# Layer 1 of the first 1024 tokens on x not divided by its rms

## The chip, the cores and the metric

The kernel runs on one core of one Trainium2 chip. The metric is the time of one execution in microseconds (us) on the device. The engines are named as in the profile: PE is TensorE's matmul, PEld its weight load, DVE is VectorE, ACT is ScalarE, POOL is GpSimd, SP is the engine whose queue issues all DMAs here.

## What is computed

Three steps follow one another, on 4 batches of 576 tokens (2304 tokens in all, 512 features):

```python
scores = q @ k.T / sqrt(64)          # 8 heads of 64
# heads 0..3: the 32 latest keys; heads 4..7: every 32nd key; both causal
x = softmax(masked(scores)) @ v      # as 2304 x 512
rms = sqrt(mean(x * x, axis=-1) + 1e-6)
xn = x / rms * rms_g
g = xn @ w_gate                      # layer 1: 512 -> 1536
x = (g * sigmoid(g) * (xn @ w_val)) @ w_out
h = x @ w_in                         # layer 2: 512 -> 2048
out = softplus(h) @ w_out2
```

Because the division by rms is one number per token, a gate product of undivided x can be divided after the product, before the sigmoid; the value product enters the result of layer 1 linearly, so its division can wait until the end of layer 1.

## The kernel before

**Layout.** x is held transposed, features on the partitions and tokens along the free axis, in `xs`. The tokens are cut into five chunks, `CUTS = (0, 512, 1024, 1536, 2048, 2304)`. Side 0 is chunks 0 and 1 (1024 tokens, `TA`), side 1 is chunks 2, 3 and 4. Layer 1 runs over side 0, then over side 1; layer 2 follows in the same order.

**Products.** Each float32 operand is split into a high part h (a ScalarE copy to fp32r) and a low part l = x - h (a subtraction on VectorE or GpSimd); a product is three matmuls, h·h, h·l and l·h, of 128x128 by 512 columns (`mm3`, L434). `split_op` splits x into the operand tile `ob` (L351, L355); `direct(c)` does that for the four feature blocks of a chunk. The weights come as 64-bit floats: `decode` loads 512 KB into one of two `raw` tiles and turns it into float32 with one ScalarE and three VectorE instructions (L370 to L376; L373 is the last reader of `raw`), `prep_in` and `prep_out` split it into `win` and `wout`.

**Layer 1 of side 0.** For each f (12 blocks of 128 of the 1536 hidden units) and each chunk, `plain` makes a gate and a value product of twelve matmuls each into two PSUM banks; `chain1` makes silu on ScalarE (L867) from the gate's bank into a tile of the ring `gv`, multiplies it on VectorE with the value's bank (L868), and `halves` splits the result into the rings `gh`/`gl`. `out1` multiplies a pair of f's with `wout` and adds into `xs` on VectorE (L901; for the first pair a ScalarE copy, L899). `combine` and `build` make the operands of side 1 (`tb`, `ob`), where some products are saved by sums of operands (`quad`).

**The statistics.** `stats(c)` squares the four feature blocks on ScalarE (L452), sums them over the partitions with four products with a matrix `ones` (L453), and makes 1/rms from Ln and Exp on ScalarE (L457, L458) and three VectorE steps (L459, L461, L462) in `ssq`. For chunks 0 and 1 `norm` then multiplies x by `rms_g` and by 1/rms on VectorE (L472), ahead of the splits. For chunks 2 to 4 the squares are gathered while the attention delivers x, `rms_g` is put on at that place, and `norm` runs after.

**The order.** All instructions are collected with their dependencies and costs by `pr.add`, and a planner (`Program.emit`, `Trial`) writes the order on each engine's queue, by due times that it works back from PE's order. It chooses VectorE or GpSimd for elementwise operations on SBUF (`two`), and ScalarE or VectorE for some copies (`evict`). There are two such plans: the first covers the attention and f = 0 to 9 of side 0 (`DEALT = 10`), the second everything after.

The attention of batches 0 and 1 is written first (`attend`, units 0 to 15). Within it, at step 12, `early` calls for the statistics of chunk 0, its splits, and the products of f = 0 for it; the products of f = 1 follow. Then come silu and the first `out1`, the table for Exp and Ln again, `stats(1)`, the table for silu, and layer 1 of chunk 1. The attention of batches 2 and 3 is a list of small steps (`steps`) that `side_a` deals out between the products of f = 0 to 9; each group of four units has one `turn`, in which ScalarE switches to the Exp table, makes the exponentials, and switches back. The second of the turns takes the statistics of chunk 2 with it.

**Rings.** `gv` has two tiles of its own; for the dealt part two more are lent to it, the two halves of `ssq` for chunks 0 and 1, which nothing needs after the division.

Of the kernel before, what the change touches and what calls it, by code (L numbers as in the profile page):

```python
# [10 lines left out]
F32 = mybir.dt.float32  # L11
# [14 lines left out]
KD = DM // 128  # L26
# [10 lines left out]
W1N, W2N = DFF // 128, DF2 // 128  # L37
DEALT = 10
LT, LT2, LV, EB = 4, 4, 5, 5
WARM = 9  # L40
# [207 lines left out]
def attn_glu_softplus(  # L248
# [16 lines left out]
    def all_of(key):  # L265
        return (key, 0, 1 << 30)
# [20 lines left out]
    def dma(kb, fn, r, w):  # L287
        pr.add("SP", 650, fn, r, w, kb=kb)
# [59 lines left out]
    def split_op(src, ksrc, slot, k, n0=0, eng="POOL"):  # L348
# [3 lines left out]
        sub(eng, n, l, src, h.bitcast(F32), [ksrc, kh], [kl])  # L352

    def two(eng, n, name, o, x, y, r, w):
        pr.add("DVE", 68 + n / 0.96, lambda: getattr(nc.vector, name)(o, x, y), r, w,  # L355
               alt=(110 + n * 2.3, lambda: getattr(nc.gpsimd, name)(o, x, y)))
# [3 lines left out]

    hold = []

    def decode(src, t, kt, keep):

        raw, kraw = raws.next()
        u, ku = cvu.next()
        words = raw.bitcast(U32).rearrange("p (n two) -> p n two", two=2)
        wlo, whi = words[:, :, 0], words[:, :, 1]
        dma(512, lambda: nc.sync.dma_start(out=raw, in_=src), hold, [kraw])
        act(512, lambda: nc.scalar.activation(t, whi.bitcast(F32), AF.Copy, scale=2.0 ** -112), [kraw], [kt])  # L370
        dve(512, lambda: nc.vector.tensor_scalar(out=u, in0=t.bitcast(U32), scalar1=0x80000000, scalar2=None,
                                                 op0=ALU.bitwise_and), [kt], [ku], True)
        dve(512, lambda: nc.vector.scalar_tensor_tensor(  # L373
            out=u, in0=wlo, scalar=29, in1=u, op0=ALU.logical_shift_right, op1=ALU.bitwise_or),
            [kraw, ku], [ku])
        dve(512, lambda: nc.vector.scalar_tensor_tensor(  # L376
            out=t.bitcast(U32), in0=t.bitcast(U32), scalar=3, in1=u,
            op0=ALU.logical_shift_left, op1=ALU.bitwise_or), [kt, ku], [kt])
        dma(256, lambda: nc.sync.dma_start(out=wk[keep], in_=t), [kt], [("wk", keep, keep + 1)])

# [59 lines left out]
    def stats(c, ring_):  # L440
# [5 lines left out]
        for i, kk in enumerate((0, 2, 1, 3) if c < 2 else (0,)):  # L446
            y, ky = r, kr
            if c < 2:
# [14 lines left out]
                                                       op0=ALU.add, op1=ALU.mult), [kr, ks], [kr])  # L463
        if c < 2:
            norm(c, "DVE")
# [12 lines left out]
    def attention(at, use):  # L478
# [5 lines left out]
        mask = at.tile([128, MW], BF16, name="mask")  # L484
        dma(100, lambda: nc.sync.dma_start(out=mask, in_=masks), [], [all_of("mask")])
        vb = ring(at, "vb", 2, [128, 9, 128])
        eb = ring(at, "eb", EB, [128, 5 * LK])
        pp = ring(at, "pp", 2, [128, 6, 128])
        pt = ring(at, "pt", 4, [128, 3 * 128])
        sq = ring(at, "sq", 2, [128, 6 * SK])  # L490
        mz = ring(at, "mz", 8, [128, 2, 6])
# [29 lines left out]
        def load_v(u):  # L521
            b, p, t0, n = units[u]
            kp, nt = (LK, 9) if p < 2 else (128, 6)
            vt, (kv, _, _) = vb.next()
            src = vl[b, p] if p < 2 else vs[b, p - 2]
            vals[u // 2] = (vt, kv)
            dma(nt * (48 if p < 2 else 50), lambda: nc.sync.dma_start(out=vt[:kp, :nt, :], in_=src), [], [all_of(kv)])

# [118 lines left out]
        def stage_v(u):  # L647
# [8 lines left out]
            for a in range(n):  # L656
                t, kt = pts[a // 3]
                for h in range(2):
                    o = (2 * (a % 3) + (h ^ (u % 2))) * nq
                    pr.add("PE", 59, lambda a=a, h=h, o=o, t=t: nc.tensor.matmul(  # L660
                        xb[64 * h:64 * h + 64, a * nq:(a + 1) * nq], lhsT=vt[r0:r1, v0 + a, 64 * h:64 * h + 64],
                        rhs=t[r0:r1, o:o + nq], start=True, stop=True), [all_of(kv), kt],
                        [kx], mode=1 if loc else 3)
# [72 lines left out]
    def steps(at, after, ring_):  # L736
# [3 lines left out]
        def turn(us, cs):  # L740
            table(EXP_LN)
            rest = [at.e(u) for u in us]
            for c in cs:
                stats(c, ring_)
            table("silu_and_others")
            for fn in rest:
                fn()
            for c in cs:
                norm(c, "POOL")

# [108 lines left out]

    def chain1(gate, val, n=CH, r4=False, eng="POOL"):  # L860
        (gb, kg), (vb_, kv) = gate, val
        if "bank" in kg[0]:
            a, ka = fk["gv"].next()
        else:
            a, ka = gb, kg
        a, gb, vb_ = a[:, :n], gb[:, :n], vb_[:, :n]
        act(n, lambda: nc.scalar.activation(a, gb, AF.Silu), [kg], [ka], True)  # L867
        dve(n, lambda: nc.vector.tensor_mul(a, vb_, a), [kv, ka], [ka])  # L868
        return halves(a, ka, n, eng, r4)
# [108 lines left out]
    with tc.manual_schedule():  # L978
# [9 lines left out]
        def direct(c):  # L988
            slots = (B11, B21) if c % 2 == 0 else (B12, B22)
            for kk in range(KD):  # L990
                x, kx = xview(kk, CUTS[c], CUTS[c + 1])
                split_op(x, kx, slots[kk // 2], kk % 2, eng="DVE" if kk % 2 or c and kk < 3 else "POOL")

        gates = {}

        def half(f, c, ring_):
            gates[f, c] = [plain(w_at(f, 0), row, c, ring_) for row in (0, 1)]

        def early():
            use.s = s_banks  # L1000
            stats(0, f_banks)
            direct(0)
            half(0, 0, f_banks)

        def prepare(f, parts, u):
# [13 lines left out]

        dma(64, lambda: nc.sync.dma_start(out=id_sb, in_=ident), [], [all_of("id")])  # L1020
        dma(2, lambda: nc.sync.dma_start(out=rg_sb, in_=rg), [], [all_of("rg")])
# [13 lines left out]
        def side_a(f, queue):  # L1035
# [4 lines left out]
            for c in (0, 1) if f > 1 else (1,):  # L1040
# [5 lines left out]
                step(queue)  # L1046
                g[f, c] = chain1(gate, val, eng="DVE" if f < DEALT else "POOL")
                drain(1 if f < W1N - 1 else 0)
# [4 lines left out]
        with ExitStack() as c2:  # L1053
# [7 lines left out]
            for f in (0, 1):  # L1061
                g[f, 0] = chain1(*gates.pop((f, 0)))
            o_banks.t = f_banks.t
# [5 lines left out]
            o_banks.keys = {}  # L1069
            table(EXP_LN)  # L1070
            stats(1, t_banks)
            table("silu_and_others")
            direct(1)
            half(0, 1, v_banks)
            tv = Ring(banks.t[2:4], "bank", 2)
            use.t = use.v = tv
            for i in (0, 1):
                fk["gv"].keys[len(fk["gv"].t)] = ("ssq", i * CH, i * CH + CH)
                fk["gv"].t.append(ssq[:, i * CH:i * CH + CH])
            queue, last_turn = steps(x, {1: (2,)}, tv)  # L1080
            o_banks.t = banks.t[4:6]
# [3 lines left out]
            prep1(DEALT, 0)  # L1085
            pr.emit()
        o_banks.t = banks.t[4:6] + banks.t[2:4]
        o_banks.keys = {i: (f"bank{i}", 0, 1 << 20) for i in (2, 3)}
# [5 lines left out]
        for f in range(DEALT, W1N):  # L1094
            side_a(f, [None, None, (last_turn,)] if f == DEALT else [])
            if f == DEALT:
                combine(*SIDES[1][:2], False)
        drain(len(todo))
        o_banks.t, o_banks.keys = banks.t[4:], {}
        build(*SIDES[1], False)  # L1100
# [117 lines left out]
```

## Time and profile before

| | us |
|---|---|
| median of 3 runs | 901.63 (901.39 to 902.55) |
| the profiled execution | 900.52 |
| its span, first to last instruction | 898.7 |
| PE busy in the span | 882.7 |
| VectorE busy | 712.9 |
| ScalarE busy | 486.1 |
| GpSimd busy | 28.1 |

The rows of the profile are read from one execution; its time is its span and what lies around it. Matmuls overlap, so a busy PE says that PE had no hole, not that it did its most.

### The profile page before, as it was taken

How to read it: one execution, taken by the hardware profiler on the slowest of the kernel's cores; microseconds unless marked ns; L12 is line 12 of the kernel's file. 1: busy time of each engine (PE TensorE's matmuls, PEld its weight loads, DVE VectorE, ACT ScalarE, POOL GpSimd, SP SyncE). 2: the span in 40 equal slices, each digit the busy share in tenths (PEclk: the TensorE clock that was granted, in tenths of full speed). 3: DMA queues.
4: the chain of work that ended last, by engine and by line, in shares of the span. 5: the costliest groups of instructions: out<-in, count | busy, mean ns of one | idle time of the engine just before them, and what ended most of it. 6: DMA issues, size and time to landing. Idle time of an engine off the chain costs nothing.

```text
span 898.7 us, 14075 instructions
## 1 busy us (share of the span) xinstructions
PE 882.7 (98%) x5320; PEld 725.7 (81%) x5320; DVE 712.9 (79%) x1349; ACT 486.1 (54%) x999; POOL 28.1 (3%) x26
## 2 busy tenths in 40 slices
PE   7899999999999999999999999999999999999998
PEld 6567777778777888888888888888888888888886
DVE  4988898998599995888988799877798456676644
ACT  5987664545364675444545567544474655434331
POOL 0000010200000000000100100000000000000000
PEclk7999999999999999999999999999999999999999
DMA  7874667363040443344553025321114111111003
GB/s 254 263 228 146 205 205 224 124 214 106 13 141 23 151 152 105 134 146 140 183 154 104 2 85 178 137 71 48 47 47 153 36 47 48 47 32 39 1 1 117
DMA packets 41858, 102.18 MB, mean 114 GB/s; under 512 B 4800, under 2 KB 5568, under 8 KB 41792
## 3 DMA queue, kind: packets, MB, share of 16 engines
q1 hardware_dynamic: 41792, 101.31, 35.5%
q8 instruction: 41, 0.67, 0.3%
q14 instruction: 25, 0.20, 0.1%
HBM read 78.74 MB, written 22.54 MB: 113 GB/s over the span
## 4 chain that ended last, share of the span: by engine, by line
PE 67%; DVE 3%; issue 0%
PE bank L434 67%; DVE xs L901 1%; DVE ob L355 0%; DVE tb L355 0%; DVE xs L355 0%; DVE win L355 0%; DVE w L355 0%; DVE ssq L355 0%; DVE glx L355 0%; DVE xs L919 0%; DVE gv L355 0%; DVE ssq L868 0%; DVE gv L868 0%; DVE gl L355 0%
## 5 line engine op out<-in xcount | busy, mean ns | idle before, releaser
L434 PE MATMUL bank<-ob,win 128*128 128x512 f32 (+1 forms) x1560 | 430.8, 360 | 2.7 <-ACT ob L351 1.8
L434 PEld LDWEIGHTS bank<-ob,win 128*128 128x128 f32 x1560 | 283.4, 188 | 55.0 <-ACT ob L351 2.2
L434 PE MATMUL bank<-tb,win 128*128 128x512 f32 x672 | 232.8, 392 | 0.0
L434 PEld LDWEIGHTS bank<-tb,win 128*128 128x128 f32 x672 | 125.4, 188 | 22.9 <-DVE xs L901 0.4
L919 DVE TENSOR_TENSOR xs<-bank,xs 128x512 f32<-128x512 f32 x126 | 86.8, 689 | 45.7 <-PE bank L434 44.4
L405 ACT ACTIVATE win<-w 128x512 fp32r<-128x512 f32 (+1 forms) x136 | 83.4, 616 | 63.9 <-PE bank L434 32.7
L355 DVE TENSOR_TENSOR win<-w,win 128x512 fp32r<-128x512 f32 (+1 forms) x134 | 89.5, 673 | 15.6 <-ACT win L405 12.6
L434 PE MATMUL bank<-wout,ghx 128*128 128x512 f32 x304 | 100.0, 390 | 0.0
L434 PE MATMUL bank<-wout,gh 128*128 128x512 f32 x272 | 90.4, 390 | 0.0
L434 PE MATMUL bank<-ghx,wout 128*128 128x512 f32 x224 | 84.1, 394 | 0.0
L434 PE MATMUL bank<-gh,wout 128*128 128x512 f32 (+1 forms) x256 | 81.3, 356 | 0.5 <-DVE xs L901 0.4
L901 DVE TENSOR_TENSOR xs<-bank,xs 128x512 f32<-128x512 f32 (+1 forms) x100 | 62.2, 628 | 8.9 <-PE bank L434 8.1
L434 PEld LDWEIGHTS bank<-wout,ghx 128*128 128x128 f32 x304 | 56.9, 188 | 11.7
L434 PEld LDWEIGHTS bank<-wout,gh 128*128 128x128 f32 x272 | 50.9, 188 | 10.6
L816 ACT ACTIVATE gv<-bank 128x512 f32<-128x512 f32 x48 | 28.4, 592 | 48.1 <-PE bank L434 47.6
L434 PE MATMUL bank<-wout,glx 128*128 128x512 f32 x152 | 53.2, 389 | 0.0
L434 PEld LDWEIGHTS bank<-gh,wout 128*128 128x128 f32 x256 | 45.5, 189 | 9.0 <-DVE xs L901 1.4
L434 PEld LDWEIGHTS bank<-ghx,wout 128*128 128x128 f32 x224 | 41.9, 188 | 8.4 <-ACT ghx L856 0.2
L434 PE MATMUL bank<-wout,gl 128*128 128x512 f32 x136 | 47.7, 389 | 0.0
L373 DVE SCALAR_TENSOR_TENSOR cvu<-raw,cvu 128x512 uint32<-128x512 uint32 x68 | 46.6, 686 | 1.0
L355 DVE TENSOR_TENSOR w<-w 128x256 f32<-128x256 f32 x109 | 45.4, 416 | 0.9
L820 DVE TENSOR_TENSOR gv<-bank,gv 128x512 f32<-128x512 f32 x48 | 32.9, 685 | 16.0 <-ACT gv L816 9.0
(131 smaller groups left out, 1211.8 us busy)
## 6 DMA issues: line engine op xcount, KB each, us to landing
raw<-w SPq DMA_DIRECT2D x68, 512.0 KB, 4.1
w<-w_kept SPq DMA_DIRECT2D x56, 256.0 KB, 2.6
w_kept<-cvtx SPq DMA_DIRECT2D x26, 256.0 KB, 3.7
cvt<-w_kept SPq DMA_DIRECT2D x26, 256.0 KB, 2.7
w_kept<-w SPq DMA_DIRECT2D x24, 256.0 KB, 4.2
qk<-qk SPq DMA_DIRECT2D x8, 601.0 KB, 5.6
w_kept<-cvt SPq DMA_DIRECT2D x18, 256.0 KB, 3.5
cvtx<-w_kept SPq DMA_DIRECT2D x18, 256.0 KB, 2.8
```

Of the source, the lines that this page charges most:

```text
L355: pr.add("DVE", 68 + n / 0.96, lambda: getattr(nc.vector, name)(o, x, y), r, w, alt=(110 + n * 2.3, lambda: getattr(nc.gpsimd, name)(o, x, ...
L373: dve(512, lambda: nc.vector.scalar_tensor_tensor(out=u, in0=wlo, scalar=29, in1=u, op0=ALU.logical_shift_right, op1=ALU.bitwise_or), [kra ...
L405: act(n, lambda: nc.scalar.activation(h, t, AF.Copy), [kt], [reg(0, o + lo, o + hi)])
L434: lambda a=a, b=b, i=i, st=st, mv=mv: nc.tensor.matmul(o, lhsT=st[a], rhs=mv[b], start=(first and i == 0), stop=(last and i == m - 1), ski ...
L816: act(CH, lambda: nc.scalar.activation(o, y[0], AF.Copy), [y[1]], [ko])
L820: dve(CH, lambda: nc.vector.tensor_add(o[0], y[0], o[0]), [y[1], o[1]], [o[1]])
L901: dve(n, lambda: nc.vector.tensor_add(x, pb, x), [kp, kx], [kx])
L919: dve(DM, lambda: nc.vector.tensor_add(x, pb, x), [kp, kx], [kx])
```

## The change

For chunks 0 and 1 (`RAW = (0, 1)`) layer 1 is computed on x times `rms_g`, not divided by rms.

- `raw_op` takes the place of `split_op` in `direct`: the high part is a ScalarE copy with `rms_g` as its scale, the low part one VectorE instruction that multiplies by `rms_g` and subtracts. `norm` isn't called for these chunks.
- `chain1` multiplies the gate by 1/rms on VectorE, from its bank into the `gv` tile, and silu works on that.
- When layer 1 of side 0 is done, eight multiplications (VectorE or GpSimd, by the planner) put 1/rms on the result in `xs`.
- In `early` the splits and the first products come ahead of the statistics of chunk 0, which use the banks `v_banks` of the attention's values in place of `f_banks`. `stats(1)` and its two table switches are taken out of the line; the statistics of chunk 1 join the first turn of batch 2. The first five steps of the list are called before f = 0.
- `ssq` is needed until the end of side 0, so it isn't lent to `gv`; two new tiles `gvx` in the attention's pool are. They end with that pool, so that `gv` has two tiles for f = 10, f = 11 and `combine`; the halves of `ssq` join it after the eight multiplications.
- The planner's costs of some DMAs and of the strided value products are changed.

```diff
+RAW = (0, 1)
...
+    def raw_op(src, ksrc, slot, k, kk):
+        (h, l), (kh, kl) = op_of(slot, k)
+        g, kg = rg_sb[:, kk:kk + 1], all_of("rg")
+        act(CH, lambda: nc.scalar.activation(h, src, AF.Copy, scale=g), [ksrc, kg], [kh])
+        pr.add("DVE", 130 + CH / 0.96, lambda: nc.vector.scalar_tensor_tensor(
+            out=l, in0=src, scalar=g, in1=h.bitcast(F32), op0=ALU.mult, op1=ALU.subtract), [ksrc, kh, kg], [kl])
...
-        dma(512, lambda: nc.sync.dma_start(out=raw, in_=src), hold, [kraw])
+        dma(340, lambda: nc.sync.dma_start(out=raw, in_=src), hold, [kraw])
...
-        dma(256, lambda: nc.sync.dma_start(out=wk[keep], in_=t), [kt], [("wk", keep, keep + 1)])
+        dma(170, lambda: nc.sync.dma_start(out=wk[keep], in_=t), [kt], [("wk", keep, keep + 1)])
...
-        if c < 2:
+        if c < 2 and c not in RAW:
             norm(c, "DVE")
...
-        dma(100, lambda: nc.sync.dma_start(out=mask, in_=masks), [], [all_of("mask")])
+        dma(140, lambda: nc.sync.dma_start(out=mask, in_=masks), [], [all_of("mask")])
...
+        gvx.update((i, at.tile([128, CH], F32, name=f"gvx{i}")) for i in RAW)
...
-            dma(nt * (48 if p < 2 else 50), lambda: nc.sync.dma_start(out=vt[:kp, :nt, :], in_=src), [], [all_of(kv)])
+            dma(nt * (31 if p < 2 else 41), lambda: nc.sync.dma_start(out=vt[:kp, :nt, :], in_=src), [], [all_of(kv)])
...
-                    pr.add("PE", 59, lambda a=a, h=h, o=o, t=t: nc.tensor.matmul(
+                    pr.add("PE", 59 if loc else 36, lambda a=a, h=h, o=o, t=t: nc.tensor.matmul(
...
             for c in cs:
-                norm(c, "POOL")
+                if c > 1:
+                    norm(c, "POOL")
...
-    def chain1(gate, val, n=CH, r4=False, eng="POOL"):
+    def chain1(gate, val, n=CH, r4=False, eng="POOL", c=None):
...
+        if c in RAW:
+            r, kr = sview(CUTS[c], CUTS[c + 1]), ("ssq", CUTS[c], CUTS[c + 1])
+            dve(n, lambda a=a, gb=gb: nc.vector.tensor_mul(a, gb, r), [kg, kr], [ka])
+            gb, kg = a, ka
         act(n, lambda: nc.scalar.activation(a, gb, AF.Silu), [kg], [ka], True)
...
+                if c in RAW:
+                    raw_op(x, kx, slots[kk // 2], kk % 2, kk)
+                    continue
...
+        def give(cs):
+            for c in cs:
+                fk["gv"].keys[len(fk["gv"].t)] = ("ssq", c * CH, c * CH + CH)
+                fk["gv"].t.append(ssq[:, c * CH:c * CH + CH])
...
         def early():
             use.s = s_banks
-            stats(0, f_banks)
             direct(0)
             half(0, 0, f_banks)
+            stats(0, v_banks)
...
-        dma(64, lambda: nc.sync.dma_start(out=id_sb, in_=ident), [], [all_of("id")])
+        dma(40, lambda: nc.sync.dma_start(out=id_sb, in_=ident), [], [all_of("id")])
...
-            table(EXP_LN)
-            stats(1, t_banks)
-            table("silu_and_others")
             direct(1)
...
+                if i in RAW:
+                    fk["gv"].keys[len(fk["gv"].t)] = (f"gvx{i}", 0, CH)
+                    fk["gv"].t.append(gvx[i])
+                    continue
...
-            queue, last_turn = steps(x, {1: (2,)}, tv)
+            queue, last_turn = steps(x, {-1: (1,), 1: (2,)}, tv)
+            step(queue, 5)
...
             pr.emit()
+            if RAW:
+                fk["gv"].t, fk["gv"].keys = fk["gv"].t[:2], {}
+                give(i for i in (0, 1) if i not in RAW)
...
         drain(len(todo))
+        for c in RAW:
+            for kk in range(KD):
+                x, kx = xv(kk, c)
+                two("POOL", CH, "tensor_mul", x, x, sview(CUTS[c], CUTS[c + 1]), [kx, ("ssq", CUTS[c], CUTS[c + 1])], [kx])
+        give(RAW)
         o_banks.t, o_banks.keys = banks.t[4:], {}
         build(*SIDES[1], False)
```

## Rows read from the trace of the kernel before

**Rows 1.** The page: engines' busy time, and the granted clock in 40 slices.

```profile
PE 882.7 (98%) x5320; PEld 725.7 (81%) x5320; DVE 712.9 (79%) x1349; ACT 486.1 (54%) x999; POOL 28.1 (3%) x26
...
PEclk7999999999999999999999999999999999999999
```

**Rows 2.** Windows: the stretch, its length, then each engine's busy us (instructions).

```profile
28.00:36.00 8.00, 6.45 (x103) 3.91 (x99) 7.07 (x20) 8.00 (x42) 0.00 (x0) 1.00 0.92 296
36.00:46.00 10.00, 7.90 (x104) 5.42 (x104) 9.96 (x26) 9.53 (x37) 0.00 (x0) 1.00 0.69 219
46.00:60.00 14.00, 12.67 (x142) 9.69 (x140) 12.39 (x35) 11.36 (x42) 0.00 (x0) 1.00 0.67 208
60.00:76.50 16.50, 15.48 (x130) 9.74 (x128) 11.99 (x22) 14.76 (x28) 0.00 (x0) 1.00 0.59 187
76.50:100.00 23.50, 23.45 (x150) 18.67 (x150) 23.13 (x52) 16.57 (x29) 1.29 (x1) 1.00 0.58 173
100.00:220.00 120.00, 119.83 (x977) 95.02 (x977) 109.90 (x222) 66.29 (x117) 12.06 (x9) 1.00 0.55 174
220.00:243.00 23.00, 22.77 (x175) 17.76 (x174) 10.62 (x19) 6.60 (x14) 0.00 (x0) 1.00 0.21 69
243.00:265.00 22.00, 21.98 (x95) 17.56 (x94) 21.47 (x36) 14.75 (x23) 1.41 (x1) 1.00 0.48 144
265.00:290.00 25.00, 24.36 (x105) 19.17 (x103) 25.00 (x47) 13.04 (x26) 1.29 (x1) 1.00 0.08 21
290.00:312.00 22.00, 21.88 (x117) 18.60 (x118) 21.88 (x44) 13.09 (x24) 1.30 (x1) 1.00 0.37 121
312.00:340.00 28.00, 28.00 (x138) 23.59 (x137) 22.63 (x44) 17.91 (x32) 0.00 (x0) 1.00 0.55 177
```

**Rows 3.** Waits of PE, 28 to 77: us in total, times, longest.

```profile
PE bank L434 <- ACT ob L351: 1.8, 2, 1.4
PE bank L453 <- ACT eb L599: 1.4, 1, 1.4
PE bank L453 <- ACT gv L452: 1.0, 2, 0.5
PE bank L637 <- DVE pp L355: 1.0, 1, 1.0
PE bank L434 <- ACT win L405: 0.5, 2, 0.4
```

**Rows 4.** Timeline of PE, 28 to 77: start, us, what, idle before.

```profile
44.40 0.73 PE L434 MATMUL bank<-ob,win 128*128 128x512 f32 x2 [1.36 <-ACT ob L351]
...
76.55 0.73 PE L434 MATMUL bank<-ob,win 128*128 128x512 f32 x2 [0.39 <-ACT ob L351]
```

**Rows 5.** Timeline of DVE, 42 to 48.

```profile
42.72 2.07 DVE L472 SCALAR_TENSOR_TENSOR xs<-xs,rg_sb,ssq 128x512 f32<-128x512 f32 x3
...
45.91 0.42 DVE L371 TENSOR_SCALAR cvu<-cvt 128x512 uint32<-128x512 uint32 x1
```

**Rows 6.** Timeline of ACT, 57 to 59.3.

```profile
57.28 1.28 ACT L291 ACT_TABLE_LOAD   x1
58.58 0.28 ACT L281 ACTIVATE xs<-bank 128x128 f32<-128x128 f32 x1
...
58.91 0.37 ACT L281 ACTIVATE xs<-bank,rg_sb 128x128 f32<-128x128 f32 x1
```

**Rows 7.** The chain that ended last: two of its 56 pieces.

```profile
264.50 0.60 DVE xs L901
...
291.31 223.95 PE bank L434 x1172
```

**Rows 8.** Timeline of all engines, 270.6 to 272.6.

```profile
270.71 1.29 POOL L356 TENSOR_TENSOR tb<-xs,tb 128x512 fp32r<-128x512 f32 x1 [12.16 <-PE bank L434]
...
271.05 1.51 DVE L355 TENSOR_TENSOR ob<-xs,ob 128x512 fp32r<-128x512 f32 x1
...
272.48 0.68 DVE L355 TENSOR_TENSOR win<-w,win 128x512 fp32r<-128x512 f32 x1
```

More of the change, by code (lines that the diff above doesn't have):

```diff
@@ L359, in sub @@
         two(eng, n, "tensor_sub", o, x, y, r, w)
-    hold = []
+    hold, gvx = [], {}
     def decode(src, t, kt, keep):
@@ L1046, in side_a @@
                 step(queue)
-                g[f, c] = chain1(gate, val, eng="DVE" if f < DEALT else "POOL")
+                g[f, c] = chain1(gate, val, eng="DVE" if f < DEALT else "POOL", c=c)
                 drain(1 if f < W1N - 1 else 0)
@@ L1061, in attn_glu_softplus @@
             for f in (0, 1):
-                g[f, 0] = chain1(*gates.pop((f, 0)))
+                g[f, 0] = chain1(*gates.pop((f, 0)), c=0)
             o_banks.t = f_banks.t
```

## The prediction

> **What bounds the kernel now.** I read the page first: PE is busy for 98% of the span, and its granted clock is 0.7 in the first of 40 slices and 0.9 or more in all others [rows 1]; from 28 us on it is 1.00, the 2.4 GHz level [rows 2]. So the time is PE's work plus the holes in it, and the question is where the holes are. The table by stretches [rows 2] answers that; the reader takes length minus PE busy, row by row. From 28 to 76.5 us PE is idle for 1.55 + 2.10 + 1.33 + 1.02 = 6.0 us. From 76.5 to 340 it is idle for 0.05 + 0.17 + 0.23 + 0.02 + 0.64 + 0.12 + 0 = 1.2 us, and behind that the chain that ended last is PE's own work [rows 7]. The change adds no matmul and takes none away (the eight products with `ones` only move), so 6 us or so is all that it can win, and all of it lies ahead of 77 us.
>
> The same table shows what could be lost. VectorE is the second engine: busy for 23.13 of 23.5 us after 76.5, for 109.90 of 120 up to 220, for only 10.62 of 23 up to 243, and for 25.00 of 25 between 265 and 290. That last stretch is where layer 1 of side 0 ends and side 1 is built, and the chain that ended last [rows 7] says the same in its own way: it is VectorE, in steps of 0.60 us, from 264.50 to 290, and PE from 291.31 on. PE loses only 0.64 us there, so the two engines are in balance: what VectorE gets in addition at that place has little cover.
>
> Then the waits of PE in the front stretch [rows 3]: 1.8 us for `ob` from ScalarE, 1.4 and 1.0 us at the products with `ones`, together 4.2 us that hang on the rms; 1.0 us for `pp` and 0.5 us for `win` do not. The timeline shows the two places of the 1.8: layer 1 of chunk 0 starts at 44.40 after 1.36 us of waiting, and that of chunk 1 at 76.55 after 0.39 [rows 4].
>
> **The change part by part.**
>
> *Statistics off the path.* Before, the products of chunk 0 stand behind squares, `ones`, Ln, Exp, three VectorE steps and four divisions, and only then the splits. Afterwards the splits read x directly, so the 4.2 us of waits have nothing left to wait for but x itself. VectorE loses the eight divisions: 2.07 us for three of them [rows 5], 0.69 us each, so 5.5 us. Four of them stand right ahead of the decoding of the next weights (45.91 in the same rows), so the win for `win` of f = 1 is at stake too, 0.5 us. The splits themselves get dearer: the subtraction with a scale costs what the division cost (0.69 for 0.60, eight times, 0.7 us), and the copy on ScalarE takes a scale per partition, which added 0.09 us to a 128x128 copy (0.37 for 0.28 [rows 6]); eight copies, 0.7 us. Both lie beside the attention's own work. The step issues no DMA of its own; on SP's queue only the next weight load is touched, whose `raw` buffer VectorE gives back at L373. I take 4.2 + 0.5 = 4.7 us off. The bounds are 6.0 (every hole closes) and 0 (the attention of batches 0 and 1, on whose last x rows chunk 1 depends, leaves the same holes a little earlier). I choose near the upper end because the waits are named one by one.
>
> *Statistics of chunk 1 in the first turn.* Two table loads of 1.28 us go [rows 6], and ScalarE was busy for 14.76 of 16.5 us there; that helps `ob` of chunk 1, which is counted already. Four products with `ones` move behind 76.5, where PE has to do them anyway. Three VectorE steps of about 0.69 us, 2.1 us, move to where VectorE has 0.37 us of slack [rows 2]. The statistics of chunk 0 now keep a bank of the attention's values (`v_banks`) from the first product to the last reader; if the other bank isn't enough, a value product of the attention is late, and `xs` of chunk 1 behind it. Nothing in the trace of before shows this; it costs 0 if ScalarE paces the attention, as it does between 28 and 36 (8.00 of 8), and at most the hole that the front has now.
>
> *One multiplication more per gate.* `chain1` for chunks 0 and 1 gets a `tensor_mul` from PSUM, 24 in all, the same form as the additions in the chain, 0.60 us a step [rows 7]: 14.4 us. Silu on ScalarE now waits for it, and behind Silu in ScalarE's queue stand copies of weights and exponentials; but Silu has until the value product is through, twelve matmuls, and the gate's bank is read no later than before by more than one VectorE step. Two of the 24 fall ahead of 76.5. Eighteen fall between 76.5 and 243: 10.8 us, with the 2.1 us moved 12.9 us, into 0.37 + 10.1 + 12.38 = 22.9 us of idle VectorE. It fits on the whole, but not in the first 23.5 us. I take 0.5 us, with 0 and 4 (the 2.1 us and three multiplications, 3.9, against no slack at all) as bounds.
>
> *The hand-over from side 0 to side 1.* Four multiplications (f = 10, 11) fall into the saturated stretch: 2.4 us. The eight multiplications of xs by 1/rms come at its end: 8 x 0.60 = 4.8 us. Together 7.2 us, on an engine that has 0.53 + 0 + 0.12 us of idle time between 243 and 312, and 5.37 us between 312 and 340 [rows 2]. What is late next: the `gv` ring gets the two halves of `ssq` back only when the eight are done, and the first copies of side 1's products go to that ring; behind these, VectorE's splits of the weights of f = 1. If the backlog can be carried to 340, 7.2 - 5.4 = 1.8 us is left; if nothing can be carried, 7.2; if the planner finds a place where PE doesn't notice, 0. I take 1.8, since PE stands at 28.00 of 28 and 21.88 of 22 while VectorE is as busy as that, that is, some lead is there. The ring is also shorter here (two tiles instead of four for f = 10, 11 and `combine`); its price isn't in any row, and it belongs to the upper bound.
>
> *Costs in the planner.* The new figures for DMAs (340 for 512 and so on) and for the strided value products add no instruction and no transfer; they only change the order, on SP's queue as on the others. No row tells its sign: 0, and up to 1 us either way.
>
> *Sum.* -4.7 + 0.5 + 1.8 = -2.4 us. The profiled execution took 900.52 us (898.7 of span and 1.8 around it), so its like would be 898.1; the median of the runs shown, 901.63, is 1.1 above it, and on that scale the forecast is **899.2 us**. About 0.2% (1.8 us) is what a measurement of this kernel can tell from no change, so the forecast is only just a gain.
>
> **The rivals.**
>
> *A: the front closes fully and the hand-over is absorbed.* 901.63 - 6.0 = 895.6. For it speaks that every hole ahead of 77 us is in reach of earlier layer-1 work; against it that `pp` and the attention's exponentials have their own chain. Chance 0.18.
>
> *B: the front gains nothing that lasts.* Between 28 and 36 ScalarE is busy for 8.00 of 8 us and VectorE between 36 and 46 for 9.96 of 10: the attention may set the moment when chunk 1's x is there, and layer 1 of chunk 0, done earlier, leaves PE idle later. Then some 2 us of the front remain against 2.3 behind it: 901.9, no change. Chance 0.22.
>
> *C, on the other side: VectorE becomes the bound at the hand-over.* Its place is the chain from 264.50 to 290; its price the whole 7.2 us; it decides as soon as more than 4.2 us (the 4.7 less the 0.5) of the 7.2 reach PE. 901.63 - 4.7 + 0.5 + 7.2 = 904.6, slower. For it: 25.00 of 25 and the shorter ring. Against it: the 5.37 us of slack after 312. Chance 0.27.
>
> *D: GpSimd takes the eight multiplications and stops VectorE.* The code lets the planner put them there. Beside one GpSimd subtraction of 1.29 us VectorE's subtraction took 1.51 us instead of 0.68 [rows 8]: 0.83 us lost each time. Eight of them cost VectorE 6.6 us where its own work would be 4.8: 1.8 us more than forecast, 901.0, no change. Chance 0.06. The Trainium skill, "SBUF — State Buffer", section "Who interferes with whom", has this as a rule: a VectorE instruction with two SBUF inputs and a GpSimd instruction that reads SBUF exclude each other for the whole instruction. By that rule GpSimd is no free place for the eight; the rows just named agree with it.
>
> **How the numbers follow.** The forecast has 0.27, A 0.18, B 0.22, C 0.27, D 0.06. The forecast and A are gains, though the forecast's own spread (some 1.5 us) puts a part of it into no change: faster 0.43, same 0.28, slower 0.29. The range reaches from A to C and a little beyond at the top for the order on the queues: 895.3 to 905.0; what is left out are the ends where both bounds of the front and of the hand-over meet. The likeliest case alone is 897.5 to 901.
>
> **What would show it.** Right: the first layer-1 products of chunk 0 start before 41 us instead of 44.40, those of chunk 1 before 73 instead of 76.55; the waits for `ob` and at the products with `ones` ahead of 77 us shrink from 4.2 to under 1 us; PE's idle time between 243 and 312 stays under 3 us. Wrong: PE idle between 243 and 312 of 5 us or more (C); PE's saturated stretch that starts no earlier than now though the products of chunk 0 do (B); or holes between 76.5 and 220, where PE has 0.2 us now, which would mean that the extra multiplications are on PE's path, through a gate bank that comes free too late.

## The result: slower, and where the time went

| | before | after |
|---|---|---|
| median of 7 runs each, us | 899.69 | 905.69 |
| ratio after / before, 95% interval | | 1.0068 [1.0046, 1.009] |
| profiled execution, us | 900.52 | 904.23 |
| its span, us | 898.7 | 902.2 |

The forecast was 899.2 us with a range of 895.3 to 905.0; the change costs 0.68%, so the sign is wrong and the time lies just beyond the range. Of the two medians of this table, the second is 6.0 us above the first, where the forecast had it 2.4 us below. The page of the kernel after, engines' busy time and the chain that ended last:

```profile
PE 879.9 (98%) x5320; PEld 723.9 (80%) x5320; DVE 719.5 (80%) x1360; ACT 480.2 (53%) x998; POOL 47.2 (5%) x38
...
PE 68%; DVE 18%; DMA 7%; ACT 4%; issue 2%; SPq 0%; DVEq 0%; ACTq 0%
PE bank L442 64%; DMA w_kept<-cvtx 3%; DVE cvu L381 2%; DVE xs L915 2%; DMA raw<-w 2%; DVE win L363 1%; PE bank L669 1%; DVE cvu L379 1%; PE bank L646 1%; DVE cvtx L384 1%; DVE w L363 1%; DVE mz L590 1%; ACT eb L608 1%; PE bank L575 1%; DMA vb<-v_loc 1%
```

The number of matmuls is that of before. New are the DMAs in the chain, 7% of the way to the end, most of it through the storing of decoded weights (`w_kept<-cvtx`) and the loading of raw ones (`raw<-w`). The chain of the kernel before, which can be followed back over 70% of the span only, had none:

```profile
PE 67%; DVE 3%; issue 0%
```

The windows of the kernel after, with columns as in [rows 2]:

```profile
28.00:36.00 8.00, 6.45 (x100) 4.96 (x94) 7.98 (x19) 7.97 (x34) 0.00 (x0) 1.00 0.91 293
36.00:46.00 10.00, 10.00 (x103) 6.91 (x102) 7.80 (x26) 8.89 (x31) 1.27 (x1) 1.00 0.32 96
46.00:60.00 14.00, 11.23 (x155) 8.99 (x152) 12.64 (x35) 12.91 (x51) 1.70 (x3) 1.00 0.95 315
60.00:76.50 16.50, 16.01 (x140) 11.87 (x139) 11.68 (x22) 13.81 (x28) 0.00 (x0) 1.00 0.50 132
76.50:220.00 143.50, 141.72 (x1159) 110.04 (x1150) 138.27 (x281) 82.42 (x147) 14.44 (x11) 1.00 0.55 175
243.00:265.00 22.00, 22.00 (x97) 17.70 (x96) 21.50 (x36) 14.12 (x22) 3.21 (x3) 1.00 0.46 132
265.00:290.00 25.00, 24.03 (x105) 18.92 (x104) 25.00 (x45) 12.47 (x23) 10.07 (x5) 1.00 0.12 32
290.00:312.00 22.00, 22.00 (x120) 19.00 (x119) 22.00 (x44) 12.88 (x25) 1.57 (x1) 1.00 0.20 53
340.00:520.00 180.00, 177.41 (x926) 150.60 (x925) 145.50 (x270) 88.77 (x160) 10.54 (x7) 1.00 0.41 126
340.00:890.00 550.00, 547.38 (x2651) 459.30 (x2650) 414.04 (x731) 273.89 (x504) 13.35 (x9) 1.00 0.27 83
```

The stretch from 340 on, in the kernel before:

```profile
340.00:890.00 550.00, 549.96 (x2675) 463.70 (x2674) 417.07 (x734) 276.62 (x503) 9.13 (x7) 1.00 0.26 81
```

Read length minus PE busy again. From 28 to 76.5 PE is idle for 4.8 us, 6.0 before. From 76.5 to 220 it is idle for 1.78 us, 0.22 before. From 243 to 312, the place that was feared, for 0.97 us, 0.78 before. And from 340 to 890, where nothing of the arithmetic was changed, it is idle for 2.62 us, 0.04 before, all but 0.03 of it ahead of 520. The holes behind 76.5 have a pattern that the forecast had no term for.

In the front the waits on the rms went as forecast. The waits of PE of the kernel after, 28 to 77, with columns as in [rows 3]:

```profile
PE bank L669 <- DMA vb<-v_loc: 2.4, 1, 2.4
PE bank L442 <- ACT eb L608: 1.1, 1, 1.1
PE bank L669 <- ACT pt L282: 0.4, 1, 0.4
PE bank L646 <- DVE pt L279: 0.3, 1, 0.3
PE bank L461 <- ACT gvx L460: 0.2, 1, 0.2
```

Of the 4.2 us that the prediction hung on the rms 0.2 is left (the last row). But a wait of 2.4 us for the attention's values has come, and 1.1 us behind an exponential (`eb`). The latter isn't quite new: in [rows 3] the 1.4 us at the products with `ones` had `eb` for their releaser too, so they didn't hang on the rms alone. The timeline of PE of the kernel after answers to [rows 4]:

```profile
33.43 1.90 PE L442 MATMUL bank<-ob,win 128*128 128x512 f32 x7 [1.09 <-ACT eb L608]
...
52.78 0.80 PE L669 MATMUL bank<-pt,vb 96*64 96x64 f32 x20 [2.44 <-DMA vb<-v_loc]
...
65.85 0.39 PE L442 MATMUL bank<-ob,win 128*128 128x512 f32 x1
```

Layer 1 of chunk 0 starts by 33.43 instead of 44.40, and that of chunk 1 at 65.85 instead of 76.55 (the products of f = 0 and 1 of chunk 0 stand ahead of it).

The new holes after 340 that the waits of PE name are three, all behind VectorE: two of 1.3 us together at L830 and one of 1.25 us at L882. The last is followed back here. This is the timeline of the kernel after, all engines, 379.9 to 388.2:

```profile
380.60 0.33 SPq L377 DMA_DIRECT2D raw<-w  x1
...
381.33 0.32 SPq L387 DMA_DIRECT2D w_kept<-cvtx  x1
...
383.88 0.63 ACT L413 ACTIVATE win<-w 128x512 fp32r<-128x512 f32 x1 [2.94 <-DMA w<-w_kept]
...
386.61 0.66 ACT L378 ACTIVATE cvtx<-raw 128x512 f32<-128x512 f32 x1 [2.10 <-DMA w_kept<-cvtx]
387.17 0.58 ACT L826 ACTIVATE gv<-bank 128x512 f32<-128x512 f32 x1
387.30 0.43 DVE L379 TENSOR_SCALAR cvu<-cvtx 128x512 uint32<-128x512 uint32 x1 [1.47 <-ACT cvtx L378]
387.64 0.42 DVE L882 TENSOR_TENSOR ssq<-bank,ssq 128x256 f32<-128x256 f32 x1
...
388.12 0.39 PE L442 MATMUL bank<-gh,wout 128*128 128x256 f32 x1 [1.25 <-DVE ssq L882]
```

SP issues the load of raw weights and, 0.73 us later, the store of the tile decoded before. ScalarE's next decoding copy (L378) may overwrite that tile only when the store has landed; it stands at the head of ScalarE's queue and waits 2.10 us. VectorE's next instruction waits for that copy (1.47 us), and behind it stands the 0.42 us multiplication (L882) that PE needs: 1.25 us of PE are lost, for a weight that is only decoded to be stored and read back later. The planner had put the copy there, as its costs had the transfers through by then.

How often ScalarE waits like that is in its waits, 300 to 520, those that a DMA ended, in the kernel after:

```profile
ACT cvtx L378 <- DMA w_kept<-cvtx: 11.7, 8, 4.8
...
ACT wout L433 <- DMA cvt<-w_kept: 7.8, 3, 3.7
ACT win L413 <- DMA w<-w_kept: 6.8, 5, 2.9
...
ACT cvt L378 <- DMA raw<-w: 3.2, 2, 2.0
```

That is 29.5 us; the same four kinds sum to 4.8 us in the kernel before (3.2, 0.2, none and 1.4).

### The profile page after: what moved, and what is told of

Its sections match the earlier page's. It is cut to its first block, busy times and chain, and to the rows that moved or that the text cites. A ratio compares the mean times of both kernels' runs of the same rounds, so it can differ in the third digit from the quotient of the medians.

```text
span 902.2 us, 14114 instructions
## 1 busy us (share of the span) xinstructions
PE 879.9 (98%) x5320; PEld 723.9 (80%) x5320; DVE 719.5 (80%) x1360; ACT 480.2 (53%) x998; POOL 47.2 (5%) x38
## 4 chain that ended last, share of the span: by engine, by line
PE 68%; DVE 18%; DMA 7%; ACT 4%; issue 2%; SPq 0%; DVEq 0%; ACTq 0%
PE bank L442 64%; DMA w_kept<-cvtx 3%; DVE cvu L381 2%; DVE xs L915 2%; DMA raw<-w 2%; DVE win L363 1%; PE bank L669 1%; DVE cvu L379 1%; PE bank L646 1%; DVE cvtx L384 1%; DVE w L363 1%; DVE mz L590 1%; ACT eb L608 1%; PE bank L575 1%; DMA vb<-v_loc 1%
## 5 line engine op out<-in xcount | busy, mean ns | idle before, releaser
L442 PE MATMUL bank<-ob,win 128*128 128x512 f32 (+1 forms) x1560 | 444.3, 362 | 2.4 <-ACT eb L608 1.1
L442 PE MATMUL bank<-tb,win 128*128 128x512 f32 x672 | 236.7, 393 | 1.4 <-DVE gv L830 1.3
L363 DVE TENSOR_TENSOR win<-w,win 128x512 fp32r<-128x512 f32 (+1 forms) x125 | 83.4, 669 | 19.3 <-ACT win L413 16.9
L830 DVE TENSOR_TENSOR gv<-bank,gv 128x512 f32<-128x512 f32 x48 | 32.9, 685 | 18.4 <-ACT gv L826 10.2
L442 PE MATMUL bank<-glx,wout 128*128 128x512 f32 x112 | 43.5, 396 | 0.0
```

The lines of the kernel that those rows point to most:

```text
L442: lambda a=a, b=b, i=i, st=st, mv=mv: nc.tensor.matmul(o, lhsT=st[a], rhs=mv[b], start=(first and i == 0), stop=(last and i == m - 1), ski ...
L830: dve(CH, lambda: nc.vector.tensor_add(o[0], y[0], o[0]), [y[1], o[1]], [o[1]])
```

## The experiments

The theory from these rows: the loss is the planner's, by the new costs of DMAs. It reckons a DMA as landed its cost times 5 ns after the one ahead of it on the queue, plus 1100 ns; 340 for a raw load means 2.8 us where 512 meant 3.66. The page's list of DMA issues of the kernel after (KB each, median us to landing) says which is nearer:

```profile
raw<-w SPq DMA_DIRECT2D x68, 512.0 KB, 4.2
```

Rivals: the 24 multiplications have taken VectorE's reserve, so that anything late is felt; or any change of costs shuffles the order by chance, and its sign means nothing. In the diffs the old line is that of the kernel after, unless it says otherwise. Each ratio is against runs of the kernel before on the same chip.

**All costs put back, and all costs alone.** The first keeps the new arithmetic with every old cost; the second is the kernel before with every new cost.

```diff
-dma(340, ... out=raw       -dma(170, ... out=wk[keep]   -dma(140, ... masks
+dma(512, ... out=raw       +dma(256, ... out=wk[keep]   +dma(100, ... masks
-31 if p < 2 else 41        -59 if loc else 36           -dma(40, ... ident
+48 if p < 2 else 50        +59                          +dma(64, ... ident
```

> The changed kernel with all the planner's costs of before (512 and 256 for the weights, 48 and 50 for the values, 100 and 64 for mask and identity, 59 for every value product); the computation is the changed kernel's. Theory P (the loss comes from the planner's new costs, which place work that waits for a DMA too early in ScalarE's and PE's queues): the waits for a landing go (2.4 us of PE at 50 us, 2.6 us of PE between 340 and 480), the time is 898 to 901 us, 0.5% or more under the changed kernel. Theory V (the loss comes from VectorE's 32 added multiplications): 904 to 907 us, as the changed kernel.

> The kernel before with the planner's new costs and nothing else. Theory P: 903 to 906 us, with PE waits behind 340 us that the kernel before doesn't have. Theory V: 899 to 901 us, no change.

Measured: 910.29 us, ratio 1.0113 [1.0094, 1.0131], and 908.38 us, 1.0093 [1.0076, 1.011]. The second lies above the 903 to 906 expected and says that the costs alone can lose more than the whole change did. The first missed under either theory: with the old costs the new arithmetic is slowest of all. Its trace has no hole behind 340 (PE busy for 549.96 of 550 us); it loses ahead of that: PE is idle for 7.3 us between 28 and 76.5, at a mean granted clock of 0.82, and for 4.8 us between 76.5 and 220. In both runs the clock has a part: the mean granted clock of their executions is 0.9895 and 0.9906, that of the kernel before on the same chip 0.9952. By the rows on the clock at the end of this document (some 4 us for 0.006) that is 3 to 4 us of their 8 to 10 us, an estimate. So the costs are two matters, and the next runs separate them.

**Weights' costs and the others apart, on the new arithmetic.** e3 puts back 512 and 256 only; e4 puts back the costs of masks, identity, values and value products only, and keeps 340 and 170.

> The changed kernel with the old costs for the weights' DMAs alone (512 and 256). Theory P: the waits between 340 and 480 us go (some 3 us), the 2.4 us at 50 us stays: 901 to 903 us. Theory V: 904 to 907 us.

> The changed kernel with the old costs for values, mask, identity and value products, and the new ones for the weights. Theory P: the wait for the value load at 50 us goes (2.4 us), those between 340 and 480 us stay: 902 to 905 us. Theory V: 904 to 907 us.

Measured: 900.05 us, 1.0000 [0.9988, 1.0012]; and 905.01 us, 1.0052 [1.0033, 1.0071]. They lie just below and at the upper end of what was expected (901 to 903 and 902 to 905). The loss goes with the weights' costs. In e3 PE is busy for 179.98 of 180 us between 340 and 520 (177.41 in the kernel after), and ScalarE's waits for the four kinds of DMA there sum to 5.1 us. PE's wait for the attention's values in the front goes with the weights' costs too, and not with the values' own: e4 still has one of 2.0 us between 40 and 60, e3 has none.

**The same two on the kernel before.** e5 gives the kernel before the new costs of masks, identity, values and value products, e6 the new 340 and 170; e7 is the new arithmetic with nearly the old figures, and e8 is the kernel after, order untouched, with the 24 multiplications cut to 16 columns (silu then reads 496 columns that they don't write, so the results are not the kernel's; the work left is the same).

```diff
 # e7
-dma(340, ... out=raw       -dma(170, ... out=wk[keep]
+dma(500, ... out=raw       +dma(250, ... out=wk[keep]
 # e8
-nc.vector.tensor_mul(a, gb, r)
+nc.vector.tensor_mul(a[:, :16], gb[:, :16], r[:, :16])
```

> The kernel before with the new planner costs for values, mask, identity and value products, the weights' costs left at 512 and 256. Theory W (what loses is the weights' new cost, and the new value costs are harmless or good): 898 to 901 us. Theory R (any change of a cost reshuffles the whole order, and the time moves by several us without a direction of its own): as well 903 or more, or 897 and less.

> The kernel before with the weights' DMAs planned at 340 and 170 and nothing else changed. Theory W: 904 to 907 us, of which 2 to 4 us are lost between 300 and 500 us, where PE waits for VectorE or ScalarE behind a weight load that has not landed. Theory R: no rule; the stretch from 300 to 500 us may be without a loss.

> The changed kernel with the weights' DMAs planned at 500 and 250, next to the 512 and 256 of before; the other new costs stay. Theory W: within 2 us of 900.05, the time at 512 and 256. Theory R: further off than 2 us, though the change of cost is 2%.

> The changed kernel, with each of the 24 gate multiplications issued on 16 of its 512 columns; the rest of the gate is left undivided. The order on every engine is the changed kernel's, so this is the price of VectorE's time for them. Theory V (VectorE's added work is on PE's path): 3 us or more under the changed kernel's 905.7. Theory W: at most 1.5 us under it.

Measured: e5 900.34 us, 0.9991 [0.998, 1.0003]; e6 903.5, 1.0033 [1.0021, 1.0044]; e7 900.65, 1.0001 [0.9991, 1.0011]; e8 902.19, 1.0019 [1.0007, 1.003]. The low weights' costs lose on the kernel before as well: 0.33%, where from e3 to the kernel after it is 0.68 (0.45 in the repeat). The place was expected between 300 and 500 us with 2 to 4 us; e6's trace has PE idle for 0.6 us between 312 and 340 and 0.6 between 340 and 520. A shift from 512 to 500, which also gives another order, moves nothing. Cutting VectorE's 24 multiplications short gives back more than half of the loss by the middle values (0.19% is left of 0.68, or of the 0.45 of the repeat below), including most of the holes after 340 (PE idle for 0.51 us between 340 and 890), where none of the 24 runs. ScalarE's waits for the four kinds of DMA between 300 and 520 are still 27.9 us, against 29.5: the same late transfers cost PE 0.51 us in place of 2.62 (1.80 in the profile of the repeat). The first rival is thus part of the answer: late transfers hurt more where VectorE has less reserve. How the shorter work ahead of 300 reaches behind 340 isn't shown.

**Which of the two weights' figures.** e9 has 340 and 256, e10 512 and 170, e11 680 and 340. e12 is another question: the new arithmetic for chunk 0 alone, with 512 and 256.

```diff
 # e12, beside 512 and 256
-RAW = (0, 1)
+RAW = (0,)
...
+            table(EXP_LN)
+            stats(1, t_banks)
+            table("silu_and_others")
...
-            queue, last_turn = steps(x, {-1: (1,), 1: (2,)}, tv)
-            step(queue, 5)
+            queue, last_turn = steps(x, {1: (2,)}, tv)
```

> The changed kernel with only the cost of keeping a weight set back (256); the load of raw weights stays at 340, and the other new costs stay. Theory K (ScalarE waits in its queue for the keeping DMA to release the decoded tile, 11.7 us in all between 300 and 520 us): most of the loss goes, 900 to 902 us. Theory L (the too early load of raw weights is what counts): 903 to 906 us.

> The changed kernel with only the cost of loading raw weights set back (512); keeping stays at 170. Theory K: 903 to 906 us, ScalarE still waits 8 us or more for the keeping DMA between 300 and 520 us. Theory L: 900 to 902 us.

> The changed kernel with the weights' DMAs planned dearer than they were before, 680 and 340. Theory W (only too low a cost hurts, as it puts the waiting instruction too early): 899 to 902 us. Theory R (the time depends on the order by chance): as likely above 902 as below.

> Chunk 0 alone undivided, with the old costs of the weights' DMAs and the other new costs; chunk 1 is divided as before, with its statistics at their old place. Twelve gate multiplications and four at the end in place of 24 and eight. Theory V (the multiplications eat up what the front gains, some 2.7 us for the 24): 897 to 899.5 us, less than both kernels. Theory F (the front gains only if chunk 1 is undivided too): 900 to 902 us.

Measured: e9 904.25 us, 1.0044 [1.0023, 1.0064]; e10 898.08, 0.9966 [0.9951, 0.9982]; e11 899.44, 0.9982 [0.9966, 0.9997]; e12 902.27, 1.0008 [0.9994, 1.0023]. It is the load: 340 loses with either figure for the store, and e10, which differs from the kernel after in that one number, is faster than both kernels. (e10 came out below the 900 to 902 of its own theory. The executions of e9 have a mean clock of 0.9914, where the kernel before has 0.9943 beside it, so some 2 us of e9's 4 may be clock, an estimate as above.) That the store, which names the worst wait, had the wrong price was a theory too, and it fell: in e10, with the store still at 170, ScalarE's wait for it falls from 11.7 to 5.3 us, and the time with it. What precedes it on SP's queue is the load. The wait hangs on both figures, though: 7.4 us in e9, and 0.6 in e3, where both are the old ones. e12 says that chunk 1 must be taken along; with chunk 0 alone nothing is gained.

**The parts of the change in the good order, and the loss again.** e13 and e14 are e10 with the 24, and with the eight multiplications, cut to 16 columns; e15 is e10 with 680 instead of 512; e16 is the kernel after once more.

```diff
 # e14
-two("POOL", CH, "tensor_mul", x, x, sview(CUTS[c], CUTS[c + 1]), ...
+two("POOL", CH, "tensor_mul", x[:, :16], x[:, :16], sview(CUTS[c], CUTS[c + 1])[:, :16], ...
```

> The changed kernel with the raw weights' load planned at 512 again, and the 24 gate multiplications issued on 16 of 512 columns (the rest of the gate stays undivided); the order on every engine is that of the kernel with 512. Theory V (the multiplications eat up the front's gain): 2 us or more under 898.1, so 896 or less, 0.55% or more under the kernel before. Theory N (they are hidden where the weights are in time, and the front's gain was small to begin with): within 1 us of 898.1, some 0.35% under the kernel before.

> The same kernel with the eight multiplications at the end of side 0 issued on 16 of 512 columns (the rest of x stays undivided); order unchanged. The prediction's term for the hand-over (1.8 us with the gate's four, 7.2 in the rival): 1 to 4 us under 898.1. Theory N: within 1 us of it, as the lag behind the kernel before does not grow between 260 and 300 us in any of the runs so far.

> The changed kernel with the raw weights' load planned at 680, keeping at 170. Theory W (only too low a cost for the load hurts): 897 to 900.5 us. Theory R (chance of the order): as likely above.

> The changed kernel once more, beside the same runs of the kernel before. Theory W: 0.4% to 0.9% slower than before, as in its first timing. If the first timing was a matter of the chip: within 0.3%.

Measured: e13 897.04 us, 0.9951 [0.9936, 0.9965]; e14 898.52, 0.9967 [0.9953, 0.9981]; e15 897.61, 0.9961 [0.9948, 0.9974]; e16 905.5, 1.0045 [1.0029, 1.0062]. The loss repeats. e13 falls between its two theories (896 or less, and within 1 us of 898.1). e15 is the best whole kernel: 0.39% under the kernel before, 3.5 us. Its windows, and its waits of ScalarE for DMAs between 300 and 520, which are one kind where the kernel after had four:

```profile
76.50:220.00 143.50, 143.45 (x1190) 112.30 (x1189) 139.00 (x286) 82.33 (x145) 12.88 (x11) 1.00 0.54 173
...
340.00:520.00 180.00, 180.00 (x950) 154.47 (x949) 152.47 (x281) 91.25 (x163) 2.98 (x2) 1.00 0.39 126
```

```profile
ACT win L413 <- DMA w<-w_kept: 2.6, 3, 1.0
```

The page of e15, the chain that ended last, has the DMAs back at 1%:

```profile
PE 86%; DVE 7%; issue 3%; ACT 3%; DMA 1%; POOL 0%; SPq 0%; ACTq 0%; DVEq 0%; POOLq 0%
```

For the 24 multiplications the window from 76.5 to 220 of e10, and of e13, where they are short, is plain:

```profile
76.50:220.00 143.50, 141.73 (x1183) 110.20 (x1182) 139.21 (x280) 82.30 (x146) 14.60 (x12) 1.00 0.55 174
```

```profile
76.50:220.00 143.50, 143.50 (x1174) 113.07 (x1167) 131.83 (x282) 82.77 (x147) 14.50 (x12) 1.00 0.56 177
```

VectorE is busy for 7.4 us less, and PE's 1.77 us of holes are gone, as 0.9966 became 0.9951 (1.4 us). The two ratios come from two chips and their intervals overlap, so the trace shows this and the times alone don't.

## Why the prediction was wrong

**The step that failed** is "Costs in the planner": "0, and up to 1 us either way", since no row told the sign. The load's cost alone is worth the difference between e10 (0.9966) and the kernel after (1.0068, and 1.0045 when repeated): 0.8 to 1.0% of 900, 7 to 9 us. On one chip it is much the same, e15 (0.9961) against the repeat (1.0045). With the store at 256 it is 4 us (e3 and e9, 0.44%), and on the kernel before the two weights' costs together lose 3.0 us (e6). A row did bear on the sign: on the page of the kernel before the raw load's median to landing is 4.1 us, close above the 3.66 us that the old 512 stands for and far above the 2.8 us of the new 340:

```profile
raw<-w SPq DMA_DIRECT2D x68, 512.0 KB, 4.1
```

I saw that the costs change the order and took a change of order for something without a direction. The timeline at 380 shows one: in a queue that is worked off in order, ScalarE's copy whose transfer was planned too early held up what stood behind it (2.10 us, of which 1.25 reached PE).

The profiles place only a part of the 7 to 9 us. PE's busy time that is left from 76.5 us to the end, at a clock of 1.00, tells how far a kernel has got by then. In the kernels before and after and in e10:

```profile
76.50:910.00 833.50, 817.10 (x4442) 677.77 (x4442) 655.08 (x1194) 424.87 (x765) 26.49 (x20) 1.00 0.32 101
```

```profile
76.50:910.00 833.50, 816.26 (x4438) 673.80 (x4428) 662.62 (x1206) 418.59 (x761) 42.64 (x28) 1.00 0.32 101
```

```profile
76.50:910.00 833.50, 814.88 (x4465) 675.40 (x4463) 665.40 (x1206) 423.97 (x762) 38.41 (x28) 1.00 0.31 101
```

The kernel after is 1.4 us behind e10 at 76.5, and behind 340 it has 2.62 us of holes where e10 has 0.36. That is about the 3.4 us by which the two profiled spans differ (902.2 and 898.8); for the rest of the timed difference no stretch is known.

**The front: the waits right, the size not.** Products of chunk 0 before 41 us and of chunk 1 before 73 were the signs given, 33.43 and 65.85 came; waits on the rms below 1 us, 0.2 came. But the holes from 28 to 76.5 show 1.2 us, 6.0 less 4.8, and not 4.7: the load of values and the exponentials were next in line. By the PE time left at 76.5 the front of the kernel after gained 0.8 us, and that of its repeat lost 1.9 (819.04 left); e10 gained 2.2, e14 3.0 (814.11), e15 2.1 (815.00) and e13 4.8 (812.33), where e10, e13 and e14 have one order and up to there differ only in the gate multiplications ahead of 76.5. So single executions scatter by 2 to 3 us, but all except e13 lie well under the term. That is nearer to rival B, in which some 2 us of the front remain, than to the term. The timed e13, where the 24 are short and the transfers planned well, is 0.49% faster, 4.4 us with an interval of 3.2 to 5.8, which looks like the 4.7; but its executions have a mean clock of 0.9958 beside 0.9940, some 1 us by the rows at the end (an estimate), it has the other new costs in it, and in e3's order the whole change gains nothing. That the front is worth 4.7 us isn't shown.

**One multiplication more per gate: right sign, too small.** 0.5 us was taken, 1.4 us (0.9966 to 0.9951) is what the times give in e10's order; the intervals overlap, so the trace's 1.77 us of holes is the better witness. Those holes are the sign that the prediction named for it. In the order of the kernel after the 24 cost more: 1.0019 in e8 against 1.0068 and 1.0045, 2.3 to 4.4 us. In e15's order PE has only 0.05 us of holes there, so the price is the order's, not the instruction's.

**The hand-over: 1.8 us taken, next to nothing measured.** e14 (0.9967) is e10 (0.9966), which by the intervals leaves room for 1.8 us either way; in the traces PE is idle for 1.41 us between 243 and 312 in both, so the eight cost nothing there. In the kernel after PE lost 0.97 us, 0.78 before: the bound of "under 3 us" was met. All eight multiplications went to VectorE, between 287.15 and 300.12, at 0.64 to 0.68 us each, so rival D, GpSimd taking them, did not come about.

**The sum.** The forecast was -2.4; e10 measures -3.1 (0.34% of 901.5), e15 -3.5, e3 and e7 nothing. That e10 comes near is partly luck: the front was taken too large, the gate's multiplications too small and the hand-over too large, and these errors go against each other. The order that came cost 7 to 9 us against e10's. Rival C named 904.6 us, near the 905.69 that came, for a reason that the runs contradict.

**What stays open.** The chance of the order isn't settled. All timings here with 340 lose (seven, of six kernels: 0.19 to 0.93%), and of the ten with 500 or more nine lie between -0.49 and +0.08%; but e1, with all the old costs, loses 1.13% ahead of 340 us. e3 and e10 differ only in the store's 256 or 170, and by 0.34%. e5 and e6 add up to 0.24% where e2, which has both edits, loses 0.93%. The clock is a part of these differences: the executions of e3 have a mean of 0.9928, those of e10 0.9944, with 0.9952 and 0.9943 for the kernel before beside them, which by the rows below is about half of the 0.34% (an estimate); and e1 and e2 have the lowest clocks of all. So the finding about the load holds for most orders tried; why an order gets the clock that it gets, and the rest of the differences, stays open.

## What to carry to other kernels

A planner's cost of a transfer is part of the kernel: change it in a run of its own, and hold it against the measured time to landing on the page first. A figure too low (340, 2.8 us for a landing of 4.1) put waiting instructions at the head of ScalarE's queue, where they held up work that has nothing to do with them; one that is too high (680, 4.5 us) cost nothing here. A stall that names one transfer (`w_kept<-cvtx`) may hang on the one ahead of it on the same queue. And a wait that is taken away is worth only what the next one in line leaves of it: 4.2 us of waits went, 1.2 us of holes.

## What was not expected of the hardware

**The total goes with TensorE's clock.** In the windows of the kernel before, and then of the kernel after, the mean granted clock from 10 to 28 us differs:

```profile
10.00:28.00 18.00, 15.87 (x303) 12.98 (x304) 13.89 (x48) 14.81 (x86) 0.00 (x0) 0.72 0.81 272
```

```profile
10.00:28.00 18.00, 12.67 (x311) 10.67 (x312) 14.25 (x48) 14.87 (x85) 0.00 (x0) 0.81 0.91 310
```

Between the levels of 1.2 and 2.4 GHz, 0.72 means 10.1 of the 18 us at the lower one, 0.81 means 6.8. Before it fell PE had been busy for 7.19 of 10 us in the one and 7.29 in the other. Of the runs of the kernel before, the 11 with a mean clock of 0.998 over the whole execution took 897.9 to 899.9 us, the 16 with 0.992 took 901.9 to 904.2. A difference of one profile to another of under 4 us can therefore be clock alone, which is why the sizes above are taken from timed comparisons where there are some; these have clocks of their own, named above where they differ.

**GpSimd beside a full VectorE.** In the timeline of GpSimd, kernel after, one subtraction of 128x512 took 5.90 us, while VectorE was busy for 25.00 of 25 us (265 to 290); the same form took 1.29 us in [rows 8]. That such spans are rough should be kept in mind.

```profile
264.89 5.90 POOL L364 TENSOR_TENSOR ob<-xs,ob 128x512 fp32r<-128x512 f32 x1 [6.36 <-ACT ob L352]
```

PE lost 0.97 us in that stretch. The Trainium skill, "SBUF — State Buffer", section "Who interferes with whom", has a VectorE instruction with two SBUF inputs contend with a GpSimd instruction that reads SBUF, over a port pair that is an exclusive lock. The long span agrees with that, but no run here takes the one engine's work away to show it.

**Stores landed later than loads of the same size.** From the list of DMA issues of the kernel after (KB each, median us to landing):

```profile
w<-w_kept SPq DMA_DIRECT2D x56, 256.0 KB, 2.7
w_kept<-cvtx SPq DMA_DIRECT2D x26, 256.0 KB, 4.0
```

The same 256 KB take 2.7 us when they are read back and 4.0 us when they are stored, half as long again (3.1 and 4.5 us for the stores from the two other tiles); the time from issue includes what stands ahead on the queue. In the planner both have one formula, 2.4 us for the store at its old figure of 256.
